# Linear attention and a sentence-level expert layer on one core: zero matmuls, products from PSUM, and a moved expert load

## The chip, the cores and the metric

The kernel runs on one core of a Trainium2 chip. The metric is the device time of one execution in microseconds, as the median of several runs. A core has a matmul engine (TensorE, in the profile PE, with its weight loads as PEld), VectorE (DVE), ScalarE (ACT), GpSimd (POOL) and a queue engine for transfers (SyncE, SP). Each works through its own instructions in program order, and semaphores order the engines among each other.

## The reference

Two stages. The first is a linear attention with a decaying state (4 batches, 8 heads, 768 steps, head size 48); the second sends each batch as a whole through the one expert of eight that its gate picks.

```python
for t in range(S):                                   # attention, all fp32
    kt, vt, rt = k[:, :, t], v[:, :, t], r[:, :, t]
    cur = einsum('bhd,bhe->bhde', u * kt, vt)
    y[:, :, t] = einsum('bhd,bhde->bhe', rt, state + cur)
    state = w * state + einsum('bhd,bhe->bhde', kt, vt)
x = y.transpose(0, 2, 1, 3).reshape(B, S, H * D)     # 4 x 768 x 384
logits = x.mean(axis=1) @ w_gate                     # 4 x 8
e = argmax(logits, axis=1); gate_w = softmax(logits)[e]
out[b] = gate_w[b] * (relu(x[b] @ w1[e]) @ w2[e])    # 384 -> 1024 -> 384
```

## The kernel before

The sequence is cut into blocks of 256 steps: three per batch, twelve in all, numbered g. Within a block the recurrence becomes matmuls: k and r are scaled by powers of the decay (`prep`), transposed (`transposes`), multiplied into a 256 x 256 score matrix (`scores`), masked to its lower triangle, and applied to v (`scores_v`), while a 48 x 48 state per head carries the past from block to block (`inter`, `st`). The diagonal term with u comes in as a sum over k times r times u (`bonus`, `add_bonus`). Each block has two halves, c = 0 and 1. `evac_y` copies the finished y out of PSUM, `backs` transposes it into the layout of the expert layer and sums it for the gate. `gate(b)` runs once per batch, after its third block, and `weights(b)` reads the chosen expert's index into a register and starts the two transfers of its weights on GpSimd's queue (1.5 MB of bf16 in all). Its matmuls become 28 jobs: 16 of `mm1` (three products of 384 columns each, then a relu) and 12 of `mm2` (four products each, a scaled copy after every second).

The order is written out by hand, and every engine keeps it. One iteration of the main loop treats block g and prepares block g+1: load of block g+4, `prep(g+2)`, the transposes of g+1, the products of g, the scores of g+1, `backs(g)`, `bonus(g+1)`, and in the last block of a batch the gate. Between these steps stand seven calls of `slot()`. From the 27th call on each gives about 1.2 jobs of the expert layer to TensorE, so that from iteration 3 on the two stages run interleaved; what is left runs after the loop, as a tail. In iterations 3, 6 and 9 `weights(b - 1)` stands behind `prep(g + 2)`, so that on GpSimd's queue the expert's transfers follow the scaling of a block.

PSUM is spread over small pools. `pp_tw` has one buffer, for the transposes of each half and, from block 3 on, for the transposed y (`xp`). `pp_at` has one buffer, for the scores. `pp_moe` has two, for the expert's products, the gate's logits and, in blocks 0 to 2, `xp`.

The steps that the change touches, by line: in `prep` k and r are scaled on GpSimd (L176), in blocks 0 to 2 partly on VectorE, and v is cast on ScalarE in blocks 0 to 2 (L197), later on GpSimd (L199). `transposes` is followed by one copy of both k and r from PSUM on ScalarE (`kr`, L213). `scores(g, 0)` issues on VectorE the products of k and r for the diagonal term (`prod`, L220), then the masking of the scores (`gt`, L239). `bonus` sums `prod` on TensorE (L252), copies the sums (`tcol`, L258) and multiplies them with v on GpSimd (`vt`, L260). The gate's pooled sum is L377, its logits L384, and the copy and the small instructions behind them L389 to L401. The expert's transfers are L411 and L415, its products L432 (`hp`) and L451 (`op`).

Of the kernel before, what the change touches and what calls it, by code (L numbers as in the profile page):

```python
# [18 lines left out]
def kernel(  # L19
# [12 lines left out]
    nc = tc.nc  # L32
# [13 lines left out]
    NB = S // L  # L46
    N = B * NB
    MID = L // 2
    AHEAD = 4

    const = ctx.enter_context(tc.tile_pool(name="const", bufs=1))
    inp = ctx.enter_context(tc.tile_pool(name="inp", bufs=AHEAD))
# [43 lines left out]
                out=uT[64 * a : 64 * a + D, :], in_=u.rearrange("(p a) d -> a d p", a=2)[a])  # L96
    wg = const.tile([128, NCT, E], FP32, tag="wg", name="wg")
    nc.scalar.dma_start(out=wg, in_=moe_w_gate.rearrange("(p ct) e -> p ct e", p=128))
    load(2)
    load(3)  # L100

    col_r = const.tile([128, 2], FP32, tag="col_r", name="col_r")
    col_k = const.tile([128, 2], FP32, tag="col_k", name="col_k")
# [41 lines left out]
    nc.vector.memset(bmask[0:64, :, 0, :], 1.0)  # L145
    nc.vector.memset(bmask[64:128, :, 1, :], 1.0)

    uwT = const.tile([128, NP], FP32, tag="uwT", name="uwT")
    U8 = const.tile([128, NP, H], BF16, tag="U8", name="U8")
    nc.vector.memset(U8, 0.0)  # L150
    wcmask = const.tile([128, NP, 2 * D], FP32, tag="wcmask", name="wcmask")
# [1 line left out]
    nc.vector.memset(ones_col, 1.0)  # L153

    def late_constants():
        nc.vector.tensor_mul(uwT, uT, wT)
        for p in range(NP):
            for a in range(2):
                q = slice(64 * a, 64 * a + 64)
                nc.vector.tensor_copy(U8[q, p, 2 * p + a : 2 * p + a + 1], uwT[q, p : p + 1])  # L160

    def late_constants2():
        lnwT = const.tile([128, NP], FP32, tag="lnwT", name="lnwT")
# [16 lines left out]
    def prep(g):  # L180
        kg, rg = raw.pop(("k32", g)), raw.pop(("r32", g))
        vb = work.tile([128, 2, H, D], BF16, tag="vb", name=f"vb{g}")
        c0, c1, cc = slice(0, 1), slice(1, 2), slice(0, 2)
        if g == 0:
            for c in (c0, c1):
                scale(nc.gpsimd, kp[g % NR], kg, dk, c)
                scale(nc.vector, rp[g % NR], rg, dr, c)
        elif g < NB:
            scale(nc.gpsimd, kp[g % NR], kg, dk, cc)
            scale(nc.gpsimd, rp[g % NR], rg, dr, c0)  # L190
            scale(nc.vector, rp[g % NR], rg, dr, c1)
        else:
            scale(nc.gpsimd, kp[g % NR], kg, dk, cc)
            scale(nc.gpsimd, rp[g % NR], rg, dr, cc)
        vsrc = raw.pop(("v32", g)).rearrange("q h c d -> q c h d")
        if g < NB:
            nc.scalar.copy(vb, vsrc)  # L197
        else:
            nc.gpsimd.tensor_copy(vb, vsrc)  # L199
        vbs[g] = vb  # L200

    def transposes(g, c):
        twp = pp_tw.tile([128, 2 * NP, 128], BF16, tag="tw", name=f"twp{g}_{c}")
        for o, src in ((0, kp[g % NR]), (NP, rp[g % NR])):
            for p in range(NP):
                nc.tensor.transpose(  # L206
                    out=twp[:, o + p, :],
                    in_=src[:, c, 2 * p : 2 * p + 2, :].rearrange("s a b -> s (a b)"),
                    identity=ident,
                )  # L210
        if c == 0:
            krs[g] = work.tile([128, 2 * NP, 2, 2, 64], BF16, tag="kr", name=f"kr{g}")
        nc.scalar.copy(krs[g][:, :, :, c, :], twp.rearrange("q o (j i) -> q o j i", j=2))  # L213

    def scores(g, rnd):
        kr = krs[g]
        if rnd == 0:
            prod = work.tile([128, NP, 2, 2, 64], BF16, tag="prod", name=f"prod{g}")
            for c in range(2):
                nc.vector.tensor_mul(  # L220
                    prod[:, :, c], kr[:, 0:NP, :, c, :], kr[:, NP : 2 * NP, :, c, :])
            gts[g] = work.tile([128, 2, 2, 2, 2, 128], BF16, tag="gt", name=f"gt{g}")
            vts[g] = prod
        at = pp_at.tile([128, 2, 2, 2, 128], FP32, tag="at", name=f"at{g}_{rnd}")
        for pp in range(2):
            p = 2 * rnd + pp
            for cs in range(2):
                for j in range(2):
                    for a in range(2):
                        q = slice(64 * a, 64 * a + D)  # L230
                        nc.tensor.matmul(  # L231
                            out=at[64 * j : 64 * j + 64, a, pp, cs, :],
                            lhsT=kr[q, p, j, cs, :],
                            rhs=kr[q, NP + p, j].rearrange("q c i -> q (c i)"),
                            start=True,
                            stop=True,
                            skip_group_check=True,
                        )
        nc.vector.tensor_mul(  # L239
            gts[g][:, rnd].rearrange("q a p c t -> q (a p) c t"),  # L240
            at.rearrange("q a p c t -> q (a p) c t"),
            mask.rearrange("q n s c i -> q n s (c i)"),
        )
# [94 lines left out]
    def evac_y(g, j):  # L338
        if j == 0:
            xns[g] = work.tile([128, 2, DM], BF16, tag="xn", name=f"xn{g}")  # L340
        if g < NB or j == 0:
            nc.scalar.copy(xns[g][:, j, :], ys[g][j][:, 0:DM])
        else:
            nc.vector.tensor_copy(xns[g][:, j, :], ys[g][j][:, 0:DM])

    def backs(g):
        b, gi = divmod(g, NB)
        if gi == 0:
            xts[b] = xpool.tile([128, NCT, S], BF16, tag="xt", name=f"xt{b}")
        xn, sp = xns.pop(g), s_ps[b]  # L350
        if g < NB:
            xp = pp_moe.tile([128, 512], FP32, tag="moe", name=f"xp{g}").bitcast(BF16)
            xp = xp[:, 0 : NCT * L].rearrange("q (t l) -> q t l", t=NCT)
        else:
            xp = pp_tw.tile([128, 2 * NP, 128], BF16, tag="tw", name=f"xp{g}")
            xp = xp.rearrange("q a b -> q (a b)")[:, 0 : NCT * L].rearrange(
                "q (t l) -> q t l", t=NCT)
        xv = xp.rearrange("q t (c j i) -> q t c j i", c=2, j=2)
        for j in range(2):
            for ct in range(NCT):  # L360
# [11 lines left out]

    gates = {}

    def gate(b):
        pooled = gpool.tile([128, NCT], FP32, tag="pooled", name=f"pooled{b}")
        nc.vector.reduce_sum(  # L377
            pooled,
            s_ps[b][:, DM : DM + NCT * 2 * NB].rearrange("q (t c) -> q t c", c=2 * NB),
            axis=AX.X,  # L380
        )
        lgp = pp_moe.tile([128, 512], FP32, tag="moe", name=f"lgp{b}")
        for ct in range(NCT):
            nc.tensor.matmul(  # L384
# [44 lines left out]
    def mm1(b, w1, ht, ft, sb):  # L429
# [5 lines left out]
                start=(ct == 0), stop=(ct == NCT - 1),  # L435
            )
        o = ht[:, ft, SB * sb : SB * sb + SB]
        if (ft * NSB + sb) % 2:
            nc.scalar.activation(out=o, in_=hp[:, 0:SB], func=ACT.Relu)  # L439
        else:  # L440
            nc.vector.tensor_scalar_max(o, hp[:, 0:SB], 0.0)  # L441

    def mm2(b, w2, ht, gw, si, half, cell, obs):
# [10 lines left out]
            )  # L454
        if half:
            ob = obs[gi]
            if si % 2:
                nc.scalar.activation(out=ob[:, c, :], in_=op[:, 0:DM], func=ACT.Copy,  # L458
                                     scale=gw[:, 0:1])
            else:  # L460
# [10 lines left out]


    SLOTS = 7
    START = NB * SLOTS + 5
    RATE = 8.5 / SLOTS
    done = [0, 0.0]

    def slot():
        done[0] += 1
        if done[0] > START:  # L480
            done[1] += RATE
            c = int(done[1])
            done[1] -= c
            moe(c)

    prep(0)
    transposes(0, 0)
    transposes(0, 1)
    prep(1)
    late_constants()  # L490
    scores(0, 0)
    scores(0, 1)
    bonus(0)
    late_constants2()
    for g in range(N):
        b, gi = divmod(g, NB)
        if g + AHEAD < N:
            load(g + AHEAD)
        if g + 2 < N:
            prep(g + 2)  # L500
        if b and gi == 0:
            weights(b - 1)
        nxt = g + 1 < N
        if nxt:
            transposes(g + 1, 0)
# [14 lines left out]
            scores(g + 1, 0)  # L520
        slot()
        backs(g)
        slot()
        if nxt:
            scores(g + 1, 1)
        slot()
        if nxt:
            bonus(g + 1)
        slot()
        if gi == NB - 1:  # L530
            gate(b)
    weights(B - 1)
    moe(len(jobs))


# [28 lines left out]
```

## Time and profile before

| | |
|---|---|
| Median of 3 runs | 180.97 us (179.42 to 181.25) |
| Profiled execution | 180.51 us |
| its span, first to last instruction | 178.8 us |
| mean granted clock of TensorE | 0.914 |
| busy: PE, PEld | 138.4 us (77%), 101.5 us (57%) |
| busy: DVE, ACT, POOL | 96.5 us (54%), 73.8 us (40%), 71.5 us (40%) |
| moved by DMA | 25.67 MB, mean 144 GB/s |

The time of an execution is a little longer than the span, which counts from the first instruction to the last. Shares are of the span. Matmuls are pipelined and their ends are modelled, so a busy PE is not one at its peak. The granted clock has two levels here, 1.0 (2.4 GHz) and 0.5 (1.2 GHz). The releaser behind an idle time is inferred from the semaphores, and each engine waits in its own order.

### The profile page before, as it was taken

To read this page: it belongs to the slowest core of one execution; us is meant where nothing else is said; L and a number is where in the kernel's file an instruction comes from. 1 tells how busy PE (TensorE), PEld (TensorE's weight loads), DVE (VectorE), ACT (ScalarE), POOL (GpSimd) and SP (SyncE) were. 2 spreads that over 40 slices of the span, in tenths; PEclk is the share of its full clock that TensorE was granted. 3 is DMA by queue.
4 is the path that set the end of the run, shared out by engine and by line. 5 is a ranking of instruction groups with operands and counts; after the bars stand their busy time and mean duration, and the time that the engine had idled before them with its cause. 6 is when DMAs were issued, how large, how long until landed. Compare 5 with 4: busy or idle time off the path is not lost.

```text
span 178.8 us, 4464 instructions
## 1 busy us (share of the span) xinstructions
PE 138.4 (77%) x1904; PEld 101.5 (57%) x1904; DVE 96.5 (54%) x200; ACT 73.8 (41%) x113; POOL 71.5 (40%) x64
## 2 busy tenths in 40 slices
PE   0041788679793299897997989889998988999992
PEld 0031657457662168675765767657576765666550
DVE  6338885765446035849474593956549434233310
ACT  0958653525051035652453447335353351234221
POOL 3244374929690084290964809277300202000000
PEclk9999999955555559999999999999999999999999
DMA  4999999996849937400059990002994002994024
GB/s 54 245 260 261 263 264 232 246 250 141 219 109 211 214 87 179 92 2 4 0 134 207 262 277 11 0 4 26 194 249 156 0 0 33 212 207 170 0 103 165
DMA packets 41604, 25.67 MB, mean 144 GB/s; under 512 B 38768, under 2 KB 39152, under 8 KB 41584
## 3 DMA queue, kind: packets, MB, share of 16 engines
q1 hardware_dynamic: 39456, 19.07, 42.6%
q0 software_dynamic: 1152, 6.29, 19.1%
q8 instruction: 15, 0.25, 0.6%
q10 hardware_dynamic: 976, 0.02, 0.3%
q14 instruction: 5, 0.04, 0.1%
HBM read 26.95 MB, written 4.72 MB: 177 GB/s over the span
## 4 chain that ended last, share of the span: by engine, by line
PE 45%; DVE 21%; DMA 17%; POOL 5%; issue 5%; ACT 2%; SPq 1%; POOLq 0%; ACTq 0%
PE hp L432 14%; PE op L451 14%; DMA w<-in_moe_w_dram 9%; DVE gt L239 7%; DVE prod L220 5%; PE twp L206 4%; DVE ht L441 4%; PE y L305 3%; DMA k<-in_k_dram 3%; DMA v<-in_v_dram 3%; PE at L231 3%; POOL rp L176 2%; DMA r<-in_r_dram 2%; POOL kp L176 2%; PE s L313 2%
## 5 line engine op out<-in xcount | busy, mean ns | idle before, releaser
L432 PE MATMUL hp<-xt,w 128*128 128x384 bf16 x192 | 42.6, 344 | 7.6 <-DMA w<-in_moe_w_dram 6.3
L260 POOL TENSOR_TENSOR vt<-vb,tcol 128x768 bf16<-128x768 bf16 x12 | 17.8, 1487 | 60.9 <-DVE tcol L258 45.3
L451 PE MATMUL op<-w,ht 128*128 128x384 bf16 x192 | 34.9, 326 | 0.7 <-ACT ht L439 0.6
L432 PEld LDWEIGHTS <-w 128*128 128x128 bf16 x192 | 25.0, 149 | 14.8 <-DMA w<-in_moe_w_dram 6.9
L213 ACT COPY kr<-twp 128x1024 bf16<-128x1024 bf16 x24 | 24.2, 1009 | 19.7 <-PE twp L206 19.6
L441 DVE TENSOR_SCALAR ht<-hp 128x384 bf16<-128x384 f32 x32 | 17.7, 554 | 26.8 <-PE hp L432 26.7
L239 DVE TENSOR_TENSOR gt<-at,mask 128x1024 bf16<-128x1024 f32 x24 | 29.3, 1220 | 5.2 <-PE at L231 4.9
L439 ACT ACTIVATE ht<-hp 128x384 bf16<-128x384 f32 x32 | 15.7, 491 | 35.2 <-PE hp L432 35.1
L176 POOL TENSOR_TENSOR kp<-k,dk 128x768 bf16<-128x768 f32 (+1 forms) x13 | 22.4, 1724 | 7.8 <-ACT dk L127 5.5
L451 PEld LDWEIGHTS <-ht 128*128 128x128 bf16 x192 | 17.3, 97 | 11.9 <-issue 1.7
L231 PE MATMUL at<-kr 48*64 48x128 bf16 x384 | 12.0, 254 | 13.4 <-DVE gt L239 12.3
L206 PE MATMUL twp<-ident,kp 128*128 128x128 bf16 x96 | 11.5, 257 | 11.3 <-POOL kp L176 9.1
L176 POOL TENSOR_TENSOR rp<-r,dr 128x768 bf16<-128x768 f32 (+1 forms) x11 | 18.8, 1707 | 0.0
L231 PEld LDWEIGHTS <-kr 48*64 48x64 bf16 x384 | 8.8, 124 | 16.5 <-issue 15.4
L305 PEld LDWEIGHTS <-gt 64*128 64x128 bf16 x384 | 13.2, 101 | 6.2 <-issue 5.2
L305 PE MATMUL y<-vb,gt 64*128 64x48 bf16 x384 | 16.1, 192 | 0.0
L206 PEld LDWEIGHTS <-kp 128*128 128x128 bf16 x96 | 8.6, 116 | 13.1 <-POOL kp L176 9.1
L461 DVE TENSOR_SCALAR ob<-op,gw 128x384 f32<-128x384 f32 x12 | 7.4, 616 | 13.2 <-PE op L451 13.2
L458 ACT ACTIVATE ob<-op,gw 128x384 f32<-128x384 f32 x12 | 7.0, 581 | 18.0 <-PE op L451 18.0
L220 DVE TENSOR_TENSOR prod<-kr 128x512 bf16<-128x512 bf16 x24 | 13.2, 586 | 1.2 <-ACT kr L213 1.1
L313 PE MATMUL s<-vb,kp 64*128 64x96 bf16 x160 | 12.7, 232 | 0.6 <-DVE st L328 0.6
L369 ACT COPY xt<-xp 128x768 bf16<-128x768 bf16 x12 | 9.6, 797 | 7.7 <-PE xp L361 7.7
(69 smaller groups left out, 157.2 us busy)
## 6 DMA issues: line engine op xcount, KB each, us to landing
w<-in_moe_w_dram POOLq DMA_DIRECT2D x8, 768.0 KB, 9.8
k<-in_k_dram SPq DMA_DIRECT2D x12, 384.0 KB, 6.1
r<-in_r_dram SPq DMA_DIRECT2D x12, 384.0 KB, 6.2
v<-in_v_dram SPq DMA_DIRECT2D x12, 384.0 KB, 6.2
out_dram<-ob SPq DMA_DIRECT2D x11, 384.0 KB, 6.6
out_dram<-ob SPq DMA_DIRECT2D x2, 192.0 KB, 1.9
wbc<-in_w_dram SPq DMA_DIRECT2D x1, 192.0 KB, 4.3
wT<-in_w_dram ACTq DMA_DIRECT2D x2, 0.8 KB, 5.4
```

Source lines behind the costliest of these rows:

```text
L176: eng.tensor_mul(dst[:, cs, :, 0:D].rearrange("q c h d -> q h c d"), src[:, :, cs, :], dec[:, :, cs, :])
L206: nc.tensor.transpose(out=twp[:, o + p, :], in_=src[:, c, 2 * p : 2 * p + 2, :].rearrange("s a b -> s (a b)"), identity=ident,)
L213: nc.scalar.copy(krs[g][:, :, :, c, :], twp.rearrange("q o (j i) -> q o j i", j=2))
L220: nc.vector.tensor_mul(prod[:, :, c], kr[:, 0:NP, :, c, :], kr[:, NP : 2 * NP, :, c, :])
L231: nc.tensor.matmul(out=at[64 * j : 64 * j + 64, a, pp, cs, :], lhsT=kr[q, p, j, cs, :], rhs=kr[q, NP + p, j].rearrange("q c i -> q (c i)") ...
L239: nc.vector.tensor_mul(gts[g][:, rnd].rearrange("q a p c t -> q (a p) c t"), at.rearrange("q a p c t -> q (a p) c t"), mask.rearrange("q n ...
L260: nc.gpsimd.tensor_mul(vt, vbs[g].rearrange("q c h d -> q (c h) d"), tcol.to_broadcast([128, 2 * H, D]))
L305: nc.tensor.matmul(out=yj[:, D * h : D * h + D], lhsT=gt[q, p // 2, a, p % 2, c, :], rhs=vb[q, c, h, :], start=(first and i == 0), stop=(c ...
L313: nc.tensor.matmul(out=sp[:, 96 * p : 96 * p + 96], lhsT=kp[g % NR][qo, c, 2 * p : 2 * p + 2, :].rearrange("s a b -> s (a b)"), rhs=vb[qo, ...
L432: nc.tensor.matmul(out=hp[:, 0:SB], lhsT=w1[:, ct, ft::NFT], rhs=xts[b][:, ct, SB * sb : SB * sb + SB], start=(ct == 0), stop=(ct == NCT - 1),
L441: nc.vector.tensor_scalar_max(o, hp[:, 0:SB], 0.0)
L451: nc.tensor.matmul(out=op[:, 0:DM], lhsT=ht[:, ft, 128 * si : 128 * si + 128], rhs=w2[:, ft, :], start=(ft == 0), stop=(ft == NFT - 1),)
```

## The change

Five things are changed together. Zero matmuls: a tile of zeros is made, 24 products of 512 of its columns stand ahead of all else on TensorE, and each call of `slot()` that brings no job of the expert layer issues one of 256 columns; their PSUM buffers are those of `pp_moe`, so `xp` goes to `pp_tw` in every block. Products from PSUM: the copy after the transposes is split, k on ScalarE and r on VectorE, and behind it VectorE multiplies k, read from PSUM, with the copied r; `scores` has no products any more. Scaling: the first block's k is scaled on VectorE, and blocks 1 and 2 are scaled by GpSimd alone. Expert loads: the pooled sum follows `backs`, the gate stands ahead of `bonus`, and `weights(b)` ends the batch's third iteration, so that it goes ahead of the next block's `prep`. Moved between engines: y is always copied by ScalarE; relu goes to ScalarE in three of four jobs instead of two, the scaled output copy in two of three. Beside these the input ring has six buffers instead of four, the expert jobs start one slot later, and the constants for the diagonal term are made without an intermediate.

```diff
-    AHEAD = 4
+    AHEAD = 6
...
-    load(2)
-    load(3)
+    for g in range(2, AHEAD):
+        load(g)
+    zero = const.tile([128, 512], BF16, tag="zero", name="zero")
+    nc.vector.memset(zero, 0.0)
+    def fill(cnt, cols):
+        for _ in range(cnt):
+            t = pp_moe.tile([128, 512], FP32, tag="moe", name="fill")
+            nc.tensor.matmul(out=t[:, 0:cols], lhsT=zero[:, 0:128], rhs=zero[:, 0:cols],
+                             start=True, stop=True)
+    fill(24, 512)
...
-        nc.vector.tensor_mul(uwT, uT, wT)
...
-                nc.vector.tensor_copy(U8[q, p, 2 * p + a : 2 * p + a + 1], uwT[q, p : p + 1])
+                nc.vector.tensor_scalar_mul(
+                    U8[q, p, 2 * p + a : 2 * p + a + 1], uT[q, p : p + 1], wT[q, p : p + 1])
...
-                scale(nc.gpsimd, kp[g % NR], kg, dk, c)
+                scale(nc.vector, kp[g % NR], kg, dk, c)
                 scale(nc.vector, rp[g % NR], rg, dr, c)
-        elif g < NB:
-            scale(nc.gpsimd, kp[g % NR], kg, dk, cc)
-            scale(nc.gpsimd, rp[g % NR], rg, dr, c0)
-            scale(nc.vector, rp[g % NR], rg, dr, c1)
...
-        nc.scalar.copy(krs[g][:, :, :, c, :], twp.rearrange("q o (j i) -> q o j i", j=2))
+            vts[g] = work.tile([128, NP, 2, 2, 64], BF16, tag="prod", name=f"prod{g}")
+        kr, tw = krs[g], twp.rearrange("q o (j i) -> q o j i", j=2)
+        nc.scalar.copy(kr[:, 0:NP, :, c, :], tw[:, 0:NP])
+        nc.vector.tensor_copy(kr[:, NP : 2 * NP, :, c, :], tw[:, NP : 2 * NP])
+        nc.vector.tensor_mul(vts[g][:, :, c], tw[:, 0:NP], kr[:, NP : 2 * NP, :, c, :])
...
-            for c in range(2):
-                nc.vector.tensor_mul(
-                    prod[:, :, c], kr[:, 0:NP, :, c, :], kr[:, NP : 2 * NP, :, c, :])
...
-        if g < NB or j == 0:
-            nc.scalar.copy(xns[g][:, j, :], ys[g][j][:, 0:DM])
-        else:
-            nc.vector.tensor_copy(xns[g][:, j, :], ys[g][j][:, 0:DM])
+        nc.scalar.copy(xns[g][:, j, :], ys[g][j][:, 0:DM])
...
-        if (ft * NSB + sb) % 2:
+        if (ft * NSB + sb) % 4:
...
-            if si % 2:
+            if si % 3:
...
-    START = NB * SLOTS + 5
+    START = NB * SLOTS + 6
...
             moe(c)
+        else:
+            fill(1, 256)
...
-    late_constants()
     scores(0, 0)
+    late_constants()
...
-        if b and gi == 0:
-            weights(b - 1)
...
         backs(g)
+        if last:
+            pool_sum(b)
...
             scores(g + 1, 1)
         slot()
+        if last:
+            gate(b)
         if nxt:
             bonus(g + 1)
         slot()
-        if gi == NB - 1:
-            gate(b)
-    weights(B - 1)
+        if last:
+            weights(b)
```

## Rows read from the trace of the kernel before

**Rows 1.** The page's slices of the span, the granted clock of TensorE in tenths.

```profile
PEclk9999999955555559999999999999999999999999
```

**Rows 2.** Table of stages: busy us (instructions) by engine, granted clock, DMA share, GB/s.

```profile
0.00:19.50 19.50, 3.65 (x56) 2.71 (x56) 10.47 (x37) 11.79 (x15) 6.72 (x15) 1.00 1.05 209
...
19.50:28.20 8.70, 6.96 (x132) 5.56 (x129) 7.07 (x10) 4.56 (x6) 4.70 (x3) 1.00 1.22 262
...
37.80:48.20 10.40, 8.75 (x132) 7.22 (x130) 5.53 (x9) 3.73 (x5) 7.46 (x5) 0.50 0.83 203
...
61.40:146.70 85.30, 78.59 (x1197) 57.66 (x1197) 51.84 (x103) 38.09 (x61) 39.83 (x30) 0.97 0.43 102
```

**Rows 3.** Order of time, TensorE: start, us, line, tile, [idle before <- releaser].

```profile
21.64 0.59 PE L206 MATMUL twp<-ident,kp 128*128 128x128 bf16 x4 [0.34 <-ACT kr L213]
...
27.35 0.64 PE L231 MATMUL at<-kr 48*64 48x128 bf16 x16 [0.75 <-DVE gt L239]
...
33.06 0.42 PE L231 MATMUL at<-kr 48*64 48x128 bf16 x16
...
36.94 0.64 PE L231 MATMUL at<-kr 48*64 48x128 bf16 x16 [2.67 <-DVE gt L239]
...
61.44 1.18 PE L432 MATMUL hp<-xt,w 128*128 128x384 bf16 x3 [5.33 <-DMA w<-in_moe_w_dram]
...
107.20 0.39 PE L206 MATMUL twp<-ident,rp 128*128 128x128 bf16 x4
...
109.23 0.39 PE L206 MATMUL twp<-ident,kp 128*128 128x128 bf16 x4
```

**Rows 4.** All waits of the span: in total, times, the longest.

```profile
PE at L231 <- DVE gt L239: 12.3, 12, 3.4
...
PE hp L432 <- DMA w<-in_moe_w_dram: 6.3, 2, 5.3
```

**Rows 5.** Order of time, ScalarE, end of the opening.

```profile
19.73 0.83 ACT L197 CAST vb<-v 128x768 bf16<-128x768 f32 x1 [0.60 <-DMA v<-in_v_dram]
```

**Rows 6.** Groups by line and shape: busy us, mean ns of one, idle before.

```profile
L213 ACT COPY kr<-twp 128x1024 bf16<-128x1024 bf16 x24 | 24.2, 1009 | 19.7 <-PE twp L206 19.6
...
L239 DVE TENSOR_TENSOR gt<-at,mask 128x1024 bf16<-128x1024 f32 x24 | 29.3, 1220 | 5.2 <-PE at L231 4.9
...
L344 DVE CAST xn<-y 128x384 bf16<-128x384 f32 x9 | 5.0, 554 | 3.1 <-PE y L268 2.9
```

**Rows 7.** Order of time, VectorE.

```profile
21.09 1.83 DVE L176 TENSOR_TENSOR rp<-r,dr 128x384 bf16<-128x384 f32 x1
...
32.88 2.87 DVE L220 TENSOR_TENSOR prod<-kr 128x512 bf16<-128x512 bf16 x2
...
48.37 0.17 DVE L389 COPY lg<-lgp 128x8 f32<-128x8 f32 x1 [1.54 <-PE lgp L384]
...
49.63 0.17 DVE L401 RECIPROCAL gw<-ssum 128x1 f32<-128x1 f32 x1
```

**Rows 8.** Single lines: durations of L220 in ns, landing times of L411.

```profile
L220 DVE TENSOR_TENSOR prod<-kr x24: 411/418/1915, 16.8 to 134.9; 128x512 bf16<-128x512 bf16 x24
...
DMA to landing us min/median/max: 6.6/7.0/8.8
```

**Rows 9.** Order of time, GpSimd, around the gate of batch 0.

```profile
46.89 1.47 POOL L260 TENSOR_TENSOR vt<-vb,tcol 128x768 bf16<-128x768 bf16 x1 [1.66 <-DVE pooled L377]
...
48.32 1.81 POOL L176 TENSOR_TENSOR kp<-k,dk 128x768 bf16<-128x768 f32 x1
...
52.61 0.72 POOL L411 DMA_DIRECT2D w<-in_moe_w_dram  x1
```

**Rows 10.** Waits of TensorE alone, 67 us to the end.

```profile
PE at L231 <- DVE gt L239: 4.0, 7, 1.0
...
PE hp L432 <- DMA w<-in_moe_w_dram: 1.0, 1, 1.0
...
PE lgp L384 <- DVE pooled L377: 0.9, 2, 0.7
```

More of the change, by code (lines that the diff above doesn't have):

```diff
@@ L146 @@
     nc.vector.memset(bmask[64:128, :, 1, :], 1.0)
-    uwT = const.tile([128, NP], FP32, tag="uwT", name="uwT")
     U8 = const.tile([128, NP, H], BF16, tag="U8", name="U8")
@@ L217, in scores @@
         if rnd == 0:
-            prod = work.tile([128, NP, 2, 2, 64], BF16, tag="prod", name=f"prod{g}")
-            for c in range(2):
-                nc.vector.tensor_mul(
-                    prod[:, :, c], kr[:, 0:NP, :, c, :], kr[:, NP : 2 * NP, :, c, :])
             gts[g] = work.tile([128, 2, 2, 2, 2, 128], BF16, tag="gt", name=f"gt{g}")
-            vts[g] = prod
         at = pp_at.tile([128, 2, 2, 2, 128], FP32, tag="at", name=f"at{g}_{rnd}")
@@ L350, in backs @@
         xn, sp = xns.pop(g), s_ps[b]
[L351 to L357, printed above, removed]
+        xp = pp_tw.tile([128, 2 * NP, 128], BF16, tag="tw", name=f"xp{g}")
+        xp = xp.rearrange("q a b -> q (a b)")[:, 0 : NCT * L].rearrange(
+            "q (t l) -> q t l", t=NCT)
         xv = xp.rearrange("q t (c j i) -> q t c j i", c=2, j=2)
@@ L373, with pool_sum @@
     gates = {}
-    def gate(b):
+    pools = {}
+    def pool_sum(b):
         pooled = gpool.tile([128, NCT], FP32, tag="pooled", name=f"pooled{b}")
@@ L381, in gate @@
         )
+        pools[b] = pooled
+    def gate(b):
+        pooled = pools[b]
         lgp = pp_moe.tile([128, 512], FP32, tag="moe", name=f"lgp{b}")
@@ L489 @@
     prep(1)
+    scores(0, 0)
     late_constants()
-    scores(0, 0)
     scores(0, 1)
@@ L496 @@
         b, gi = divmod(g, NB)
+        last = gi == NB - 1
         if g + AHEAD < N:
```

## The prediction

> **What bounds the kernel now.** I read the page first, then a table of stages, then the waits, then single engines in order of time. The stages are cut at the starts of the loop's iterations: the opening (0 to 19.5 us), iterations 0 to 3, iterations 4 to 11, and a tail.
>
> The clock line [rows 1] shows the lower level from about 36 to 67 us. The table of stages [rows 2] says the same, 0.50 in iteration 2, but also 1.00 for the opening and iteration 0, and there the durations disagree: the 16 score products take 0.64 us at 27.35 and again at 36.94 (granted 0.50), but 0.42 at 33.06 [rows 3]. So I take it that TensorE ran at 1.2 GHz through nearly all of the first 67 us, rose to 2.4 GHz near 33 us after several dense microseconds, and fell again after the idle gap of 2.67 us that ends at 36.94. A busy engine alone did not raise it: iteration 2 is 8.75 us busy of 10.4 and stays at 0.50 [rows 2].
>
> Which waits end last there? TensorE idles 12.3 us in all before score products, on the masked scores of VectorE, and 6.3 before expert products, on the expert's weights, 5.3 of it once [rows 4]. The second is the point at which the early part ends: expert 0's first product starts at 61.44, when its weights land [rows 3]. All that iterations 0 to 3 gain counts only as far as it brings that landing forward. Behind it (61.4 to 146.7) TensorE is busy 78.6 of 85.3 us, with VectorE at 51.8 and ScalarE at 38.1 [rows 2]: TensorE is the bound, and only its 6.7 idle microseconds are to be had. The tail is expert products back to back.
>
> **The change, part by part.** The profiled execution took 180.51 us, 1.71 more than its span of 178.8; the median of the three runs is 180.97, 0.46 above it. My sum goes against 180.5.
>
> *Opening.* The first block's k is scaled on VectorE instead of GpSimd, 24 zero products of 512 columns go ahead of the first transpose, the kr copy is halved, and the small constants lose their separate product. This could save 1 to 2 us before iteration 0, but it is stopped by something untouched: ScalarE's cast of block 2's v waits for its DMA until 19.73 and takes 0.83 [rows 5], and the kr copy of iteration 0 stands behind it in program order. That copy, 1.01 for 1024 elements [rows 6], is halved: at least 0.50, with its fixed part some 0.6. So the transposes that waited for it until 21.64 [rows 3] can start near 21.2: 0.45 us. If the zero products ran at the lower clock throughout they would end after the first block is scaled, but still inside the slack before 19.7: nothing. The larger ring of six input buffers issues the same loads in the same order; nothing here.
>
> *Iteration 0.* Half of block 2's r scaling leaves VectorE, where it stood from 21.09 to 22.92, 1.83 us [rows 7], ahead of a state product that TensorE waits for. It goes to GpSimd, which has slack there. With the score wait (below), I take 0.9.
>
> *Products of k and r from PSUM.* Today two of them stand in VectorE's queue between the scores and the masking, reading SBUF. One costs 0.41 at best, 0.42 in the median, 1.9 at worst [rows 8]; the worst pair (32.88, 2.87 us) makes the wait of 2.67 us at 36.94 [rows 7, 3]. The change issues copy and product straight behind the transposes, long before the scores are there. What is next late is the masking itself, 1.22 us [rows 6], less the transposes of y that TensorE does beside it: a residue that I estimate at 0.4. So iteration 1 wins 2.2; iteration 2, where the product ran early already, nothing.
>
> Not seen before is VectorE copying, or multiplying, 512 bf16 elements out of PSUM. Bounds: 0.41 (the product from SBUF) and, on the line through 0.55 for 384 and 1.22 for 1024 fp32 elements from PSUM [rows 6], 0.69; below the first I exclude a gain, as no instruction of that count went faster. I take 0.55 each, the middle, as no row is nearer to either. This time lies beside work of TensorE; VectorE's load in the steady iterations hardly changes, since the y copy (9 of 0.55 [rows 6]) and a share of the relu and output copies go to ScalarE, which idles 47 us there.
>
> The Trainium skill speaks against this edit ("VectorE: DVE Perf Modes", Rules for kernel authors): on a matmul's output accept the slow rate, or copy to SBUF first if many operations follow. Its section "Why PSUM operands drop a tier" still allows bf16 the packed rate. By the first the price would be the 0.69, by the second nearer 0.41; no row here decides, and the sum is the same with either, since the time is beside other work. The page "SBUF — State Buffer" (its section on engine ports and the shared pair) says that a VectorE instruction with two SBUF inputs is locked out while GpSimd reads SBUF. The long pair at 32.88 agrees, as GpSimd was scaling then; by that page a product with one PSUM input can't be held so, and the 1.9 would not return.
>
> *Zero products in the slots.* Seven of 256 columns per iteration up to slot 27. Three expert products of 384 columns take 1.18 us at the lower clock [rows 3], so one filler is at most 0.26 there, and about half at the upper level. Five of the seven stand in waits, two on the path: 0.2 to 0.5 per iteration, 0.8 in total for iterations 1 and 2. What they buy is the clock. The evidence is thin: dense work raised it once (33 us) and failed to in iterations 2 and 3, so what the fillers add may well tip it; from 67 us on it stays up [rows 1], with waits of 1 us at most. At 0.42 for 0.64 TensorE's stretches shrink by a third; of an iteration of 8 to 9 us about 6 is TensorE on the path and the rest VectorE, so 2.0 per iteration, 4.0 for iterations 1 and 2. Bounds: 0 and 6.
>
> *Expert loads ahead of the scaling.* Today the load of expert 0 waits behind kp, rp and the v cast and is issued at 52.61, though GpSimd was done with its vt at 48.36 (46.89 and 1.47) [rows 9]: 4.25 us. Against it: the gate's small instructions on VectorE (48.37 to 49.80, 1.4 [rows 7]) now precede the copy that vt waits for, 1.6 with a handoff. Net 2.6. Behind the load wait kp (1.81), rp and v of block 5, delayed by the issue of two transfers (0.72 the first [rows 9]); they are due an iteration later, and the weight wait covers them; without that cover they would cost at most about 1.4. The transfer lands in 6.6 to 8.8 us [rows 8]; six input buffers keep inputs flowing beside it, so I take 8.8, the longest of the four.
>
> First expert product: 0.45 + 0.9 + 2.2 + 4.0 - 0.8 + 2.6 = 9.4 us earlier, at 52.0. Iteration 3 then starts near 41.5 and ends near 47.5, so TensorE still waits some 4 us for weights: what iteration 3 gains itself is worth nothing.
>
> *Steady iterations.* From 67 us TensorE waits 4.0 for masking, 1.0 for expert 1's weights, 0.9 for the gate's pooled sum [rows 10]: 5.9. The products and the y copy leave VectorE's queue ahead of the masking; the load and the pooled sum come earlier. Next late is VectorE's release of the transposes' only PSUM buffer, now read three times. I take 4.5 of 5.9. The tail stays.
>
> Sum: 180.5 - 9.4 - 4.5 = 166.6 us.
>
> **Rivals.** *The clock stays low* in iterations 0 to 3. For it: iterations 2 and 3, dense and at 0.50. Then 4.0 go and the fillers cost 0.8 more: 166.6 + 4.8 = 171.4. Against it: one rise in that stretch already, without any fillers.
>
> *VectorE holds the transposes' buffer.* In the steady state 1.6 us of TensorE's work lie between the first half's transposes (to 107.59) and the second's (109.23) [rows 3]. Copy and product at 0.69 each make 1.4; behind a relu or another 384-element instruction, 0.55 to 0.9 late, they end 0.7 over. Over eight iterations that is 5.6, and some 2 of the early gain: 174.
>
> *Slower than before.* The same buffer as the new bound: copy and product start 1.6 us late, behind a masking (1.22) and part of a relu. TensorE then waits 1.4 in each iteration. With the clock low and fillers of 0.5 that eats the early gain (3 x 1.9 = 5.7 against 0.45 + 0.9 + 2.2 + 2.6 = 6.2), and the steady iterations lose 8 x 1.4 = 11 and win 5.9: 180.5 - 0.5 + 5.1 = 185. It passes the time of before from about 1 us of lateness. Against it: VectorE idles 40% of the steady stage.
>
> *Better than forecast.* The weights land in 6.6, the clock gives 6, the steady waits go entirely: 180.5 - 9.4 - 2.2 - 2.0 - 5.9 = 161.0.
>
> **How the numbers follow.** Forecast, 163 to 169.5: 0.46. Clock low, 169.5 to 173: 0.22. Buffer held, 172 to 178.5: 0.10. Better, 157 to 163: 0.14. Slower, over 182.3: 0.05. No change within 1%: 0.03. The range from 159 to 174 leaves out the last two, most of the held buffer and the end of the better case. About 1% is what a measurement of this kernel tells from no change (its three runs spread by that). Faster by over 1%: 0.92; within: 0.03; slower: 0.05.
>
> **What would show it.** Right: score products of 0.42 in iterations 1 to 3; no wait over 0.5 for masking behind 30 us; the expert load issued near 43 and the first expert product near 52, with a wait for weights ahead of it; the second transposes of iteration 0 near 21.2. Wrong: durations of 0.64 up to the first expert product (clock), waits of transposes for the copy or product on VectorE (buffer), or a landing over 9 us (inputs in its way). Most uncertain is the clock, then the landing.

## The result, and the profile after

The changed kernel takes 162.76 us (median of 4 runs, 161.94 to 164.56) beside 181.11 for the kernel before in the same comparison; the ratio is 0.90, with an interval from 0.890 to 0.910. The forecast was 166.6 in a range from 159 to 174. The profiled execution took 163.36 us with a span of 161.7.

The page's clock line, to be held against [rows 1]:

```profile
PEclk9995579999996599999999999999999999999999
```

It falls at about 12 us, is up again by 24, and falls once more for two slices near 50 us. Before, this line showed seven slices down, and the durations put most of the first 36 us, where the line is high, at the lower level too. The stages, in stretches that only roughly follow the iterations (columns as in [rows 2]):

```profile
0.00:19.50 19.50, 12.22 (x101) 6.50 (x103) 12.58 (x42) 12.17 (x17) 5.40 (x14) 0.81 0.94 233
19.50:28.00 8.50, 6.99 (x157) 5.32 (x151) 6.27 (x13) 3.02 (x6) 6.26 (x4) 0.84 1.10 299
28.00:36.00 8.00, 6.74 (x168) 5.43 (x166) 5.40 (x11) 3.42 (x6) 6.99 (x6) 1.00 1.00 265
36.00:48.00 12.00, 8.51 (x201) 6.71 (x197) 9.32 (x22) 4.68 (x9) 9.74 (x9) 1.00 0.95 229
48.00:58.00 10.00, 5.51 (x70) 3.87 (x72) 1.97 (x4) 1.85 (x4) 6.46 (x5) 0.66 1.04 242
...
67.00:130.00 63.00, 61.95 (x985) 45.85 (x982) 38.65 (x84) 33.64 (x67) 31.50 (x25) 1.00 0.38 90
```

The interleaved stage is full: 61.95 busy of 63. TensorE in order of time, the rows that answer to [rows 3]:

```profile
8.45 0.40 PE L213 MATMUL twp<-ident,kp 128*128 128x128 bf16 x4
...
16.14 0.64 PE L237 MATMUL at<-kr 48*64 48x128 bf16 x16 [1.32 <-DVE gt L245]
...
18.05 0.59 PE L213 MATMUL twp<-ident,kp 128*128 128x128 bf16 x4
...
20.66 0.61 PE L213 MATMUL twp<-ident,kp 128*128 128x128 bf16 x4 [0.30 <-DVE prod L224]
...
24.88 0.42 PE L237 MATMUL at<-kr 48*64 48x128 bf16 x16 [0.60 <-DVE gt L245]
...
25.66 0.38 PE L213 MATMUL twp<-ident,kp 128*128 128x128 bf16 x4
...
31.67 0.42 PE L237 MATMUL at<-kr 48*64 48x128 bf16 x16 [0.66 <-DVE gt L245]
...
32.45 0.38 PE L213 MATMUL twp<-ident,kp 128*128 128x128 bf16 x4
...
38.77 0.73 PE L389 MATMUL lgp<-wg,pooled 128*128 128x8 f32 x6
...
39.67 0.38 PE L213 MATMUL twp<-ident,kp 128*128 128x128 bf16 x4
...
46.16 0.42 PE L237 MATMUL at<-kr 48*64 48x128 bf16 x16 [0.70 <-DVE gt L245]
...
52.49 1.18 PE L437 MATMUL hp<-xt,w 128*128 128x384 bf16 x3 [5.52 <-DMA w<-in_moe_w_dram]
```

The starts of iterations 0 to 3 before, and among them the gate's logits at the end of iteration 2:

```profile
19.53 0.59 PE L206 MATMUL twp<-ident,kp 128*128 128x128 bf16 x4
...
28.17 0.59 PE L206 MATMUL twp<-ident,kp 128*128 128x128 bf16 x4
...
37.75 0.59 PE L206 MATMUL twp<-ident,kp 128*128 128x128 bf16 x4
...
46.88 1.45 PE L384 MATMUL lgp<-wg,pooled 128*128 128x8 f32 x6 [1.18 <-DVE pooled L377]
...
48.19 0.59 PE L206 MATMUL twp<-ident,kp 128*128 128x128 bf16 x4
```

The four transposes at 8.45 take 0.40, at 20.66 0.61: the zeros had raised the clock before the first real product, and it was lost in the gaps of the opening. From 23 us on score products take 0.42. Iterations 0 to 3 start at 18.05, 25.66, 32.45 and 39.67 (before: 19.53, 28.17, 37.75 and 48.19), and the wait of 2.67 us is one of 0.66. The first expert product starts at 52.49, still behind a wait for weights, of 5.5 us. All waits of the span, to be held against [rows 4]; the second line is new:

```profile
PE hp L437 <- DMA w<-in_moe_w_dram: 5.5, 1, 5.5
...
PE twp L213 <- DVE prod L224: 5.0, 5, 2.2
...
PE at L237 <- DVE gt L245: 3.8, 5, 1.3
```

VectorE, ScalarE and GpSimd (against [rows 5], [rows 6], [rows 8] and [rows 9]): first the groups, then GpSimd at the first expert load, then the durations of the product's line in ns (least, median, most).

```profile
L222 ACT COPY kr<-twp 128x512 bf16<-128x512 bf16 x24 | 14.0, 584 | 27.6 <-PE twp L213 27.5
...
L223 DVE COPY kr<-twp 128x512 bf16<-128x512 bf16 x24 | 10.2, 425 | 19.1 <-ACT kr L222 19.0
L224 DVE TENSOR_TENSOR prod<-twp,kr 128x512 bf16<-128x512 bf16 x24 | 10.2, 424 | 0.8
```

```profile
41.55 1.48 POOL L266 TENSOR_TENSOR vt<-vb,tcol 128x768 bf16<-128x768 bf16 x1 [2.17 <-DVE tcol L264]
43.10 0.72 POOL L416 DMA_DIRECT2D w<-in_moe_w_dram  x1
...
44.37 1.82 POOL L187 TENSOR_TENSOR kp<-k,dk 128x768 bf16<-128x768 f32 x1
```

```profile
L224 DVE TENSOR_TENSOR prod<-twp,kr x24: 423/424/426, 11.5 to 116.7; 128x512 bf16<-128x512 bf16 x24
```

All 24 products lie between 0.423 and 0.426 us; none was held up, although 20 of them lie beside an instruction of GpSimd. This one lies wholly inside the `vt` at 41.55:

```profile
41.89 0.42 DVE L224 TENSOR_TENSOR prod<-twp,kr 128x512 bf16<-128x512 bf16 x1
```

The load is issued at 43.10, ahead of kp. Behind the first expert product TensorE's waits (against [rows 10]) come to little:

```profile
PE hp L437 <- ACT ht L444: 0.6, 1, 0.6
PE hp L437 <- DVE lg L394: 0.3, 1, 0.3
```

### The profile page after: what moved, and what is told of

Read it like the earlier page. It is cut to its first block, busy times and chain, and to the rows that moved or that the text cites. A ratio compares the mean times of both kernels' runs of the same rounds, so it can differ in the third digit from the quotient of the medians.

```text
span 161.7 us, 4579 instructions
## 1 busy us (share of the span) xinstructions
PE 138.3 (86%) x1955; PEld 98.5 (61%) x1955; DVE 85.9 (53%) x195; ACT 76.9 (48%) x142; POOL 70.1 (43%) x62
## 4 chain that ended last, share of the span: by engine, by line
PE 66%; DMA 12%; DVE 9%; ACT 6%; SPq 3%; issue 2%; POOLq 0%; POOL 0%
PE hp L437 20%; PE op L456 20%; PE twp L213 7%; DMA w<-in_moe_w_dram 6%; PE at L237 4%; PE y L311 4%; DMA k<-in_k_dram 4%; DVE gt L245 3%; DMA r<-in_r_dram 3%; SPq L76 3%; ACT ht L444 2%; ACT kr L222 2%; PE s L319 2%; DVE kr L223 2%; PE y L284 2%
## 5 line engine op out<-in xcount | busy, mean ns | idle before, releaser
L444 ACT ACTIVATE ht<-hp 128x384 bf16<-128x384 f32 x48 | 23.6, 492 | 15.3 <-PE hp L437 14.4
L222 ACT COPY kr<-twp 128x512 bf16<-128x512 bf16 x24 | 14.0, 584 | 27.6 <-PE twp L213 27.5
L187 POOL TENSOR_TENSOR kp<-k,dk 128x768 bf16<-128x768 f32 x11 | 20.0, 1817 | 8.6 <-ACT kr L222 8.6
L223 DVE COPY kr<-twp 128x512 bf16<-128x512 bf16 x24 | 10.2, 425 | 19.1 <-ACT kr L222 19.0
L187 POOL TENSOR_TENSOR rp<-r,dr 128x768 bf16<-128x768 f32 x11 | 20.0, 1816 | 0.0
L463 ACT ACTIVATE ob<-op,gw 128x384 f32<-128x384 f32 x16 | 9.3, 582 | 20.4 <-PE op L456 19.4
L446 DVE TENSOR_SCALAR ht<-hp 128x384 bf16<-128x384 f32 x16 | 8.9, 556 | 18.7 <-PE hp L437 18.5
L109 PE MATMUL fill<-zero 128*128 128x256 bf16 (+1 forms) x51 | 15.0, 374 | 1.4 <-DVE zero L104 1.4
L347 ACT CAST xn<-y 128x384 bf16<-128x384 f32 x24 | 11.1, 478 | 6.0 <-PE y L284 3.9
L466 DVE TENSOR_SCALAR ob<-op,gw 128x384 f32<-128x384 f32 x8 | 4.9, 617 | 14.7 <-PE op L456 14.7
```

The source lines that it names most:

```text
L109: nc.tensor.matmul(out=t[:, 0:cols], lhsT=zero[:, 0:128], rhs=zero[:, 0:cols], start=True, stop=True)
L187: eng.tensor_mul(dst[:, cs, :, 0:D].rearrange("q c h d -> q h c d"), src[:, :, cs, :], dec[:, :, cs, :])
L222: nc.scalar.copy(kr[:, 0:NP, :, c, :], tw[:, 0:NP])
L223: nc.vector.tensor_copy(kr[:, NP : 2 * NP, :, c, :], tw[:, NP : 2 * NP])
```

## The experiments

Most kernels are the changed one with one part undone or varied; three are the kernel before with one or two parts alone. Times are medians; "first expert product" is its start in the profile, and "the rest" the span behind it (before 61.44 and 117.36, after 52.49 and 109.21).

**No zeros.** Both kinds of zero products are left out.

```diff
-        for _ in range(cnt):
+        for _ in range(0):
             t = pp_moe.tile([128, 512], FP32, tag="moe", name="fill")
```

Expected: 

> The changed kernel with no zero products at all; everything else stays. My theory (the zeros buy the clock in iterations 1 and 2): score products of 0.64 us in most of iterations 0 to 3, the first expert product about 4 us later than 52.5, the time 162.8 + 4 to 5 = 167 to 168. Rival (the other edits make the early iterations dense enough to raise the clock alone, the zeros are ballast): first expert product within 1 us of 52.5 or earlier, the time 161.5 to 163.5.

Measured: 165.49 us, ratio to before 0.914 (0.900 to 0.927); first expert product at 53.83, rest 109.9. The rows are two score products of iteration 1, the second of iteration 2, and the first expert product:

```profile
31.52 0.64 PE L237 MATMUL at<-kr 48*64 48x128 bf16 x16
...
33.49 0.42 PE L237 MATMUL at<-kr 48*64 48x128 bf16 x16 [0.75 <-DVE gt L245]
...
39.79 0.42 PE L237 MATMUL at<-kr 48*64 48x128 bf16 x16 [0.51 <-DVE gt L245]
...
53.83 1.18 PE L437 MATMUL hp<-xt,w 128*128 128x384 bf16 x3 [4.42 <-DMA w<-in_moe_w_dram]
```

Both theories are half right. Without zeros the clock rises too, but near 33 us instead of 23. That costs 1.3 us at the first expert product, where I had put 4.0 less 0.8. In the time it is 1 to 3 us; the interval overlaps that of the changed kernel, so the size is not settled more closely. Nor do the zeros bring the clock up by 24 us in every execution: in the profiles of two later experiments that keep them (the loads behind the scaling, the division of the copies) the transposes at 26.15 and 26.27 still take 0.63.

**Products from SBUF, at their old place.** The copy is whole on ScalarE again, the products stand ahead of the masking.

```diff
-        nc.scalar.copy(kr[:, 0:NP, :, c, :], tw[:, 0:NP])
-        nc.vector.tensor_copy(kr[:, NP : 2 * NP, :, c, :], tw[:, NP : 2 * NP])
-        nc.vector.tensor_mul(vts[g][:, :, c], tw[:, 0:NP], kr[:, NP : 2 * NP, :, c, :])
+        nc.scalar.copy(krs[g][:, :, :, c, :], twp.rearrange("q o (j i) -> q o j i", j=2))
...
         if rnd == 0:
+            for c in range(2):
+                nc.vector.tensor_mul(
+                    vts[g][:, :, c], kr[:, 0:NP, :, c, :], kr[:, NP : 2 * NP, :, c, :])
```

Expected: 

> The changed kernel with the kr copy whole on ScalarE again and the products of k and r read from SBUF ahead of the masking, as before the change. My theory (the products in VectorE's queue ahead of the masking are what TensorE waited for): waits of score products for the masking come back, 2 to 3 us before the first expert product and 3 to 4 behind it, the time 167 to 169. Rival (the gain of the steady iterations comes from moving the y, relu and output copies to ScalarE): waits of under 2 us in all, the time under 165.

Measured: 173.77 us, 0.966 (0.958 to 0.974), 10 to 11 us slower than the changed kernel and more than either theory said. First expert product at 57.64, rest 114.0. The product's group, and the wait for masking:

```profile
L227 DVE TENSOR_TENSOR prod<-kr 128x512 bf16<-128x512 bf16 x24 | 34.1, 1457 | 1.2 <-ACT kr L221 1.1
```

```profile
PE at L237 <- DVE gt L245: 17.7, 8, 3.9
```

A product takes 1457 ns in the mean, against 424 after the change and 586 before it. The wait for masking is 17.7 us, more than the 12.3 of before [rows 4].

**Products from SBUF, at their new place.** The one operand is changed, nothing else moves.

```diff
-        nc.vector.tensor_mul(vts[g][:, :, c], tw[:, 0:NP], kr[:, NP : 2 * NP, :, c, :])
+        nc.vector.tensor_mul(vts[g][:, :, c], kr[:, 0:NP, :, c, :], kr[:, NP : 2 * NP, :, c, :])
```

Expected: 

> The changed kernel with the product issued at its new place, right behind the copies, but with both factors read from SBUF (k from ScalarE's copy, r from VectorE's). Theory A (what the change gained here is the place in VectorE's queue): no product over 0.6 us matters, the time 162 to 164.5. Theory B (it is the operand from PSUM: with two SBUF inputs the product is held while GpSimd works): products of 1 us and more again beside GpSimd's scaling in iterations 0 to 3, later masking, the time 165.5 or more. I hold the place for two thirds of it and the operand for a third.

Measured: 170.50 us, 0.948 (0.942 to 0.954): theory B, and the one for which I had given a third. First expert product at 55.02, rest 113.8. VectorE and GpSimd in the same stretch, then what TensorE waited for:

```profile
47.50 4.85 DVE L224 TENSOR_TENSOR prod<-kr 128x512 bf16<-128x512 bf16 x1
52.27 0.54 DVE L334 TENSOR_TENSOR st<-s,wcmask 128x384 bf16<-128x384 f32 x1
```

```profile
47.72 1.82 POOL L187 TENSOR_TENSOR kp<-k,dk 128x768 bf16<-128x768 f32 x1
49.49 1.80 POOL L187 TENSOR_TENSOR rp<-r,dr 128x768 bf16<-128x768 f32 x1
51.24 0.82 POOL L206 CAST vb<-v 128x768 bf16<-128x768 f32 x1
```

```profile
52.87 0.31 PE L364 MATMUL s<-ones_col,xn 128*128 128x1 bf16 x6 [2.49 <-DVE st L334]
```

One product of 512 elements lasts from 47.50 to 52.35. It ends 0.3 us after GpSimd's three instructions in a row (scaling of k, of r, the cast of v; to 52.06), and the state product behind it in VectorE's queue is late for TensorE by 2.49 us. So the operand from PSUM is what pays most, some 7 us; the place in the queue, together with the split copy, pays the other 3.

**Loads behind the scaling again.** Gate and pooled sum stay early.

```diff
         if g + 2 < N:
             prep(g + 2)
+        if b and gi == 0:
+            weights(b - 1)
...
-        if last:
-            weights(b)
+    weights(B - 1)
     moe(len(jobs))
```

Expected: 

> The changed kernel with each expert's load behind the next block's scaling again; gate and pooled sum stay early. My theory: the load of expert 0 is issued 4 us later (near 47.3), lands with less input traffic beside it, so the first expert product is 2.5 to 4 us later; expert 1 costs up to 1 us; the time 165.5 to 167.5. Rival (the load's landing is set by the inputs in the transfer queues, not by its issue): first expert product within 1 us of 52.5, the time within 1 us of 162.8.

Measured: 168.48 us, 0.936 (0.929 to 0.943); first expert product at 58.02, rest 111.2. The issue of the first load, and TensorE's waits for weights:

```profile
48.66 0.72 POOL L416 DMA_DIRECT2D w<-in_moe_w_dram  x1
```

```profile
PE hp L437 <- DMA w<-in_moe_w_dram: 9.5, 2, 8.7
```

The load is issued at 48.66 instead of 43.10 and the first expert product follows, 5.5 us later; 1.4 of that is a gate that ran later in this execution, with the lower clock into iteration 1. Mine of the two theories, and by more than I gave it; but the load still took 9.3 us to land, so the thinner input traffic that I expected beside it did not come.

**Four input buffers.**

```diff
-    AHEAD = 6
+    AHEAD = 4
```

Expected: 

> The changed kernel with four input buffers instead of six. My theory (the ring of six does nothing for the blocks, and its loads lie beside the first expert's load, which took 9.3 us to land): the load lands in 7 to 8.5 us, the first expert product comes 1 to 2.3 us earlier, the time 160.5 to 162. Rival (the blocks need the deeper ring now that iterations take 6.8 us): GpSimd waits for inputs in iterations 1 to 3, the first expert product 1 us later or more, the time 164 or more.

Measured: 160.79 us, 0.895 (0.886 to 0.903); first expert product at 49.68, the load landed in 6.6 us, sooner than either theory said. The same edit once more, beside the unaltered kernel, with more runs:

Expected of the unaltered: 

> The changed kernel once more, unaltered, as the yardstick for the next one: 162 to 164.

Expected of the four buffers: 

> The changed kernel with four input buffers once more, beside the unaltered one. My theory (fewer input transfers beside the first expert load): first expert product 2 to 3 us earlier than in the yardstick, the time 1.5 to 2.5 us below it. Rival (the first look was chance, as the intervals overlapped): within 1 us.

Measured: unaltered 163.75 us, 0.908 (0.901 to 0.915); four buffers 162.08, 0.904 (0.897 to 0.910). The first expert products of the two:

```profile
53.51 1.18 PE L437 MATMUL hp<-xt,w 128*128 128x384 bf16 x3 [6.24 <-DMA w<-in_moe_w_dram]
```

```profile
49.70 1.18 PE L437 MATMUL hp<-xt,w 128*128 128x384 bf16 x3 [1.49 <-DMA w<-in_moe_w_dram]
```

The loads are issued at 43.40 and 43.00 and land, by these rows, some 10 and 6.7 us later. Between 43.1 and 46 us all transfers together move 70 GB/s with four buffers and 250 with six (80 and 218 in the first look and in the profile after); with four no input is issued from 39.8 to 46.1. So it is the inputs beside the load that differ. In the two comparisons the first expert product comes 2.8 and 3.8 us earlier. The medians are 2.0 us lower (against the result above, from another comparison) and 1.7 (side by side), the ratio of the second by 0.004, which is 0.8 of 181 us; the intervals overlap. So the earlier landing is shown, and the gain of the time, some 1 to 2 us, only likely. By the medians this kernel and the next are the fastest that were run.

**Four buffers and a later start of the expert jobs.**

```diff
-    AHEAD = 6
+    AHEAD = 4
...
-    START = NB * SLOTS + 6
+    START = NB * SLOTS + 9
```

Expected: 

> The changed kernel with four input buffers and the expert jobs starting three slots later, so that TensorE works on iteration 4 while expert 0's first weights are on the way. My theory: the wait of 2 us for weights goes, three to four more jobs are left to the tail at 0.6 us each, all of it TensorE's work in either place; the time 158.5 to 160.5. Rival (what is shifted to the tail costs as much there as the wait did, since the tail's products wait for their two PSUM buffers): 160.5 to 162.

Measured: 161.16 us, 0.895 (0.885 to 0.905); first expert product at 52.30, rest 106.5, against 49.68 and 108.8 with four buffers alone: the wait of 2 us for weights is gone and the span is the same within 0.3. The time is the rival's; of its reason 1.1 us of new waits for VectorE's relu, which releases these buffers, can be seen, 0.7 of it behind 126 us.

**The division of the copies as before.**

```diff
-        nc.scalar.copy(xns[g][:, j, :], ys[g][j][:, 0:DM])
+        if g < NB or j == 0:
+            nc.scalar.copy(xns[g][:, j, :], ys[g][j][:, 0:DM])
+        else:
+            nc.vector.tensor_copy(xns[g][:, j, :], ys[g][j][:, 0:DM])
...
-        if (ft * NSB + sb) % 4:
+        if (ft * NSB + sb) % 2:
...
-            if si % 3:
+            if si % 2:
```

Expected: 

> The changed kernel with the copies of y, the relu and the scaled output copies divided between ScalarE and VectorE as before. My theory (these moves only keep VectorE's load level): TensorE's waits for masking rise by 1 to 2 us behind the first expert product, since the second y copy stands ahead of the masking again; the time 163.5 to 165.5. Rival (the division is what freed the steady iterations): 4 us or more, 167 upwards.

Measured: 163.81 us, 0.912 (0.907 to 0.918); first expert product at 53.52, rest 110.6. At most 1.4 us in the rest, in a profile that lies 2.0 us above the median. No score product waits for masking there; in place of the waits I named, 1.6 us of expert products wait for ScalarE's relu. The time is in my range and the rival is out, but the interval overlaps those of the changed kernel (162.76 and 163.75), so that even the sign is not settled, and the waits are not those I named.

**The kernel before, with the products from PSUM alone.** Its `transposes` and `scores` are those of the changed kernel; the products' buffer comes from there too.

```diff
-        nc.scalar.copy(krs[g][:, :, :, c, :], twp.rearrange("q o (j i) -> q o j i", j=2))
+        kr, tw = krs[g], twp.rearrange("q o (j i) -> q o j i", j=2)
+        nc.scalar.copy(kr[:, 0:NP, :, c, :], tw[:, 0:NP])
+        nc.vector.tensor_copy(kr[:, NP : 2 * NP, :, c, :], tw[:, NP : 2 * NP])
+        nc.vector.tensor_mul(vts[g][:, :, c], tw[:, 0:NP], kr[:, NP : 2 * NP, :, c, :])
...
-            for c in range(2):
-                nc.vector.tensor_mul(
-                    prod[:, :, c], kr[:, 0:NP, :, c, :], kr[:, NP : 2 * NP, :, c, :])
```

Expected: 

> The kernel before with one part of the change alone: the kr copy halved between ScalarE and VectorE and the product of k and r taken from PSUM behind the transposes. My theory: waits for masking fall from 12.3 to about 4 us, the first expert product comes 3 to 4 us earlier, the steady iterations win 3; the time 180.5 - 6 to 7 = 173 to 175. If the parts only pay together (the expert load behind the scaling hides what the early iterations gain): 177 or more. If the undoing of this part (10.5 us) is its worth alone too: 169 to 171.

Measured: 176.37 us, 0.983 (0.975 to 0.992): 3.7 us, where I had said 6 to 7; it lies between my range and the 177 of the second theory. First expert product at 59.31, rest 113.8. The waits for masking fell to 5.1 us, and iterations 1 and 2 together are 3.6 us shorter than before.

**The kernel before, with the order of gate and loads alone.**

```diff
-        if b and gi == 0:
-            weights(b - 1)
...
         backs(g)
+        if gi == NB - 1:
+            pool_sum(b)
         slot()
...
+        if gi == NB - 1:
+            gate(b)
         if nxt:
             bonus(g + 1)
         slot()
         if gi == NB - 1:
-            gate(b)
-    weights(B - 1)
+            weights(b)
```

Expected: 

> The kernel before with the order of the gate and the expert loads alone changed: pooled sum behind the transposed y, gate ahead of the diagonal sums, load ahead of the next block's scaling. If a part is worth the same alone as its undoing cost (5.7 us): 174 to 175. My theory by now, that parts depend on each other: the load of expert 0 is issued about 2.6 us earlier, but the next block's scaling then moves beside the products of k and r, which with two SBUF inputs are held while GpSimd works; a gain of 0 to 3 us, 177 to 180, with a mean product over 0.7 us (0.55 before).

Measured: 178.23 us, 0.994 (0.989 to 1.000). First expert product at 57.72, 3.7 us earlier, but rest 118.7, longer than before. Products of the block that follows the load, then TensorE's wait:

```profile
51.88 4.08 DVE L220 TENSOR_TENSOR prod<-kr 128x512 bf16<-128x512 bf16 x2
```

```profile
57.14 0.64 PE L231 MATMUL at<-kr 48*64 48x128 bf16 x16 [4.36 <-DVE gt L239]
```

The scaling, pushed behind the load, now runs from 50.99 to 55.3, beside the products, and they take 4.08 us for two. The mean product is 0.82 (0.59 before). What the load wins, the products lose for the most part.

**The kernel before, with both.** The edits are the two above together.

Expected: 

> The kernel before with both: the products from PSUM and the early gate and loads. If the two depend on each other as I hold, together they win clearly more than the sum of each alone: 10 us or more, 168 to 171, with every product at 0.42 us and the first expert product near 56. Rival (the two simply add): 180 - 3.7 - the gain of the order alone, 174 to 176.

Measured: 168.43 us, 0.937 (0.929 to 0.944): 12 us, where the two alone give 3.7 and 2.6 at most. All products are at 0.42. (Its profiled execution took 3.4 us more than the median, with transposes of 0.59 and more through the early iterations; its starts are not used.)

## Why the prediction was right, point by point

The time falls into the range, 3.8 us below the forecast and just inside the band from 157 to 163, to which I had given 0.14. It did not come there in the way given for that band: the weights landed in 9.3 us, not in 6.6. By starts in the profile, the first expert product comes 8.95 us earlier, forecast 9.4; the rest is 8.15 us shorter, forecast 4.5. That the early part came out so near is luck in part, since terms that were mis-sized made up for each other; the rest is where the difference lies.

*Opening and iteration 0*: iteration 1 starts 2.5 us earlier, 1.5 by the opening, forecast 0.45, and 1.0 by iteration 0, forecast 0.9. The cast of block 2's v, which I took for an untouched limit, ran at 17.68 already; this profile moves inputs faster from the start (233 GB/s in the opening, 209 in [rows 2]). That is not chance. Between 5 and 15 us the four profiles of the kernel before and of its variants move 253 to 263 GB/s, the ten of the changed kernel and of its variants 281 to 315, with four input buffers and without the zeros too, and in the same comparisons. So the faster inputs come with the change, and neither from the ring alone nor from the zero products alone; which part brings them was not tried. What was late next was VectorE's small constants, and then the one buffer of the transposes: 0.30 us at 20.66, which is the rival's wait in small.

*Iterations 1 and 2* together are 6.0 us shorter (6.79 and 7.22 against 9.58 and 10.44), forecast 2.2 + 4.0 - 0.8 = 5.4. The sum nearly held and its parts did not. Some 1.4 of the 6.0 belong to the gate (next point). Without the zeros the two iterations take 1.0 us more, and the first expert product comes 1.3 later: not 3.2, because the denser iterations raise the clock on their own, only later. The products gave 3.6 (alone, in the kernel before) to 4.3 (undone, at the old place), not 2.2. In part that is the clock: with the products alone and no zeros the transposes at 37.12 take 0.38, before 0.59 at 37.75. How it divides between the clock and the collisions with GpSimd that no longer happen was not separated.

*The load* is issued 3.4 us behind the start of iteration 3, before 4.4: 1.0 us, where I had 2.6. The rest of that term lies in iteration 2: TensorE no longer waits there for the pooled sum (1.18 us at 46.88 before, nothing at 38.77). With the order alone, iteration 2 is 1.4 us shorter (9.08 against 10.44) and the load 1.2 nearer to the start of iteration 3, together the 2.6. With the early gate already there, putting the load behind the scaling costs about the 4.25 that I had read from GpSimd's rows (5.5, of which 1.4 lies in the clock). The landing took 9.3 instead of 8.8. "Inputs in its way" stands in the forecast as a sign against it, and it is what happened: with four buffers the load lands in 6.6. That the larger ring does nothing was the step that was wrong: by the inputs that it lets run beside the load it delays the landing by about 3 us, and it likely costs 1 to 2 of them in the time.

*Copy and product from PSUM* take 0.425 and 0.424, the lower bound, not the middle. Of the Trainium skill's two sentences the trace bears out the one in "VectorE: DVE Perf Modes", Why PSUM operands drop a tier (bf16 keeps the packed rate), and not the advice in its Rules for kernel authors to accept the slow rate or to copy first.

*Why the product pays* is where my reasoning fell short. I wrote that it leaves the queue ahead of the masking. The experiment at the new place shows that the place, with the split copy, wins about 3 us of the 10 to 11, and that the operand wins some 7: with two SBUF inputs one product lasted 4.85 us beside GpSimd's scaling, with one PSUM input none was over 0.426. I had cited the Trainium skill for it ("SBUF — State Buffer", the engine ports and the shared pair) and then priced it at nothing, since the product in the trace of before was mostly clear of GpSimd (0.42 in the median [rows 8]). That held only as long as the other parts stayed as they were: the order alone brings the scaling beside the products (0.82 in the mean), and all the other parts together more so (1.46). In the time the order alone wins 2.6 at most and the products alone 3.7; both together 12. A part that keeps a stall away cannot be priced from a trace in which another part still keeps it away.

*The rest* is 8.15 shorter, forecast 4.5 out of 5.9 us of waits. TensorE's idle time behind the first expert product fell from 11.7 (117.36 less 105.64 busy) to 5.3 (109.21 less 103.88), 6.4 in all: the waits that I counted went nearly whole, and some small ones that I had not counted. Another 1.8 is busy time, which I had left out when I wrote that only the idle time was to be had: the lower clock lasts 3.8 us there instead of 5.3, and the diagonal sums of block 4 no longer stand behind the first expert product. VectorE held the transposes' buffer 5.0 us in five waits, all ahead of the first expert product, none behind it: that rival lives only where no expert product covers it. Its early part did come, 1.5 us in iterations 0 to 2 where I had given it some 2. That no wait for masking over 0.5 would remain behind 30 us was too strict: 0.66 at 31.67 and 0.70 at 46.16.

What stays open: which part of the change makes the inputs of the opening faster, and the zeros' worth in the time within 1 to 3 us. Which of the zeros matter, those of the opening or those of the slots, was not tried.

## What to carry to other kernels

Look at what a vector instruction reads, and what the other engine on the same memory does at that moment, before pricing its place in a queue: an operand left in PSUM cost nothing in rate here and took the product out of the conflict with GpSimd. When a change moves work on one engine, list the instructions of the other engines that it will newly run beside; two edits that each win little can win much together, and undoing one part of a change then measures more than adding it alone. A deeper ring of input buffers is not free when its loads run beside a load that everything waits for.

## What the runs showed of the hardware that was not expected

VectorE's product of two SBUF operands was held not for one instruction of GpSimd but for three in a row, 4.85 us. VectorE read bf16 from PSUM as fast as from SBUF (0.424 against 0.41 to 0.42 for 512 elements). Products on zeros raised TensorE's clock: the four transposes behind them took 0.40 us, and 0.61 without them. In the changed kernel the same 0.75 MB load took 6.6 us to land with four input buffers and 8.9 to 10.1 with six (five profiles in which TensorE waited for it); in the kernel before, with four buffers and inputs on their way beside it, 8.8.
